# Turning x by a VectorE transpose of reloaded quarters instead of TensorE transposes, in a fused convolution and token-mixing kernel

## Chip, cores and metric

The kernel runs on one core of one Trainium2 chip. The metric is the device time of the core in microseconds (us), from the medians of several executions. Every execution that is used here was of the fast kind (no core at a reduced clock for the whole run), so all times can be compared.

## The reference

A causal convolution of seven taps along the tokens, one filter for each of eight channel groups, gives x. A channel product gives angles theta, their cosine and sine make a complex z, the tokens are mixed with two 4224x4224 weights, and a gated channel product ends it.

```python
# x: (8, 4224, 192); w: softmax of weight (8 heads, 7 taps)
x = causal_conv(x, w)                       # along the 4224 tokens
theta = x @ w_theta                         # 192 x 192
zr, zi = x * cos(theta), x * sin(theta)
y = einsum('ts,bsd->btd', w_tok_r, zr) + einsum('ts,bsd->btd', w_tok_i, zi)
u = x + y
out = u + maximum(u @ w_ch, 0)
```

## The kernel before

Tokens are cut into 33 chunks of 128. Only 11 chunks of z fit on the chip at a time, so the token mixing makes three passes over the outputs, and chunks 11 to 32, called the later chunks, are made in twelve *transition steps*, six in each of the two changes from pass to pass. There are 58 steps in all; a step mixes the live chunks into two blocks of 128 output tokens. It has seven runs of matmuls named `y` (seven products of half-width blocks in place of eight), and "position 3" in a step means "at the start of its fourth run". The work of a new chunk is slipped between the `y` matmuls at such positions. TensorE takes its instructions in program order, so what is slipped in must be ready when its turn comes.

The parts that the change touches (cuts are marked `# ...`):

```python
class Chunk:
    def conv(self, j):
        # ... 8 matmuls into pc, evicted into self.x (128 x 1536, by batch and channel)
        if j == 1:
            for a in range(NQ):                       # x is also kept in DRAM
                nc.sync.dma_start(out=xs[t0 : t0 + Q, :],
                                  in_=self.x[a * Q : (a + 1) * Q, :])

    def transpose(self, g):                           # 6 TensorE transposes, ACT evicts
        self.xT[g] = transposed(self.x[:, g * GC : (g + 1) * GC], ...)

    def theta(self, g):                               # 8 matmuls v, then Sin twice
        v = channel_mix(self.xT[g], wth)
        # ...

    def tasks(self):                                  # of one later chunk, in order
        # conv 0, conv 1, transpose 0, transpose 1, theta 0, theta 1, products, sums

class Step:
    def wtile(self):                                  # turned and summed weights
        return wpool.tile([P, NW, NQ, Q], F16, name="wt", tag="wt", bufs=11)

    def output(self, i, g):                           # out = u + relu(u @ w_ch)
        u = self.pv[i][:, g * GC : (g + 1) * GC]
        ub = u.rearrange("p (k n) -> p k n", k=2)
        dve(nc.vector.scalar_tensor_tensor(
            out=ub, in0=channel_mix(self.uT[i, g], wch), scalar=0.0, in1=ub,
            op0=ALU.max, op1=ALU.add))
        nc.sync.dma_start(out=out[...], in_=u...)     # leaves from pv itself

def step_events(t):
    # ...
    if t + 4 < NSTEP and steps[t + 4].late:           # x added into part, in DRAM
        for i in range(len(steps[t + 4].tbs)):
            found.append((3.3 + 1.7 * i, lambda i=i: steps[t + 4].add_ahead(i)))
    # ...
            pos = [0, .5, 1.3, 1.6, 2.1, 2.5, 3.1, 3.15, 3.4, 3.6]   # of tasks()
            # ... one chunk, then at += 2.3 for the second of the step
```

## Time and profile before

| | before |
|---|---|
| time, median | 1480.96 us of 3 runs (1479.57 to 1488.54) |
| span of the profile | 1482.4 us |
| start, to the first convolution of a later chunk | 108.4, then 315.0 us of pure token mixing |
| first transition (T1), 423.4 to 576.4 | 153.0 us |
| middle run of token mixing | 295.9 us |
| second transition (T2), 872.3 to 1020.0 | 147.7 us |
| rest, with the outputs | 462.4 us |

The lengths of stretches are differences of times in the timeline: a transition runs from its first convolution `pc` to its last theta matmul `v`.

The profile page of before, from its parts on busy time, on slices (a fortieth of the span each; digits are tenths, PEclk is the clock granted to TensorE) and on the chain that ended last:

```profile
PE 1434.0 (97%) x10095; PEld 904.5 (61%) x10095; DVE 859.6 (58%) x914; ACT 467.3 (32%) x597; POOL 522.2 (35%) x769
...
PE   7789999999999999999999999999999999969997
...
PEclk9999999999999999999999999999999999989999
...
PE 88%; DMA 4%; ACT 3%; DVE 2%; issue 1%; POOL 1%; SPq 0%; DVEq 0%; ACTq 0%; POOLq 0%
```

TensorE (PE) is busy 97% of the span, and the chain of work that ended last is 88% TensorE. VectorE (DVE) is busy 58% of the time. The one weak slice after the start, a 6 in the last third, is a gap. TensorE's waits in the whole of before (microseconds in all, times, longest):

```profile
engine line waited for: us in total, times, longest us
PE y L430 <- ACT pv L393: 14.5, 2, 13.7
...
PE v L138 <- ACT z L233: 3.0, 9, 0.6
```

The gap is the first line's 13.7 us, at 1321 us: a `y` product waits for ScalarE's eviction into `pv`, and ScalarE in turn waits 19.8 us for an output DMA that still reads the old `pv`.

The timeline of TensorE in before, in the first transition step (start, microseconds, engine, line, operation, operands, count):

```profile
425.61 0.52 PE L196 MATMUL pc<-xw,bands 96*64 96x192 f16 x8
...
428.35 0.50 PE L153 MATMUL tp<-ident,z 128*128 128x128 f16 x6
428.69 1.14 PE L430 MATMUL y<-z,wt 128*128 128x384 f16 x6
...
431.30 0.82 PE L138 MATMUL v<-wth,uT 128*128 128x192 f16 x8
```

Theta follows the end of the convolution's matmuls by about 5 us. And six transposes, given as 0.50 us, delay the next `y` by only 428.69 - 428.35 = 0.34 us, since matmuls overlap.

The same transitions in the table of stretches (stretch, length, busy time of each engine with its count, mean granted clock, share of the DMA engines, GB/s):

```profile
core 0: us, PE busy (x) PEld busy (x) DVE busy (x) ACT busy (x) POOL busy (x), PEclk, DMA share, GB/s
423.40:576.40 153.00, 153.00 (x1217) 98.50 (x1217) 95.35 (x117) 86.00 (x110) 56.26 (x93) 1.00 0.96 162
872.30:1020.00 147.70, 147.22 (x1181) 94.84 (x1181) 92.81 (x114) 84.02 (x108) 55.85 (x91) 1.00 1.02 172
```

The DMA share is the sum of the times of all packets over that of the 16 engines, so it can pass 1. In both stretches TensorE is busy with hardly a pause (0.5 us in the second) at full clock, and the DMA share is about 1.

### The profile page before, as it was taken

What the parts mean: (1) busy time and instruction counts of PE and PEld (TensorE: products, weight loads), DVE (VectorE), ACT (ScalarE), POOL (GpSimd) and SP (SyncE); (2) the same over time, 40 slices, a digit from 0 to 9 for tenths busy, and PEclk for the clock granted to TensorE, in tenths of its full rate; (3) what the DMA queues carried; (4) which work ended last, traced back from release to release, by engine and by line L of the source; (5) the groups of instructions that cost most, each with busy time, mean ns of one, the idle gap of its engine ahead of it and who ended that gap; (6) DMA issues with size and microseconds to landing.
All of it is one profiled execution on the core that took longest, in us unless ns stands there. A gap on an engine that the chain in (4) does not pass through costs nothing.

```text
span 1482.4 us, 24605 instructions
## 1 busy us (share of the span) xinstructions
PE 1434.0 (97%) x10095; PEld 904.5 (61%) x10095; DVE 859.6 (58%) x914; ACT 467.3 (32%) x597; POOL 522.2 (35%) x769
## 2 busy tenths in 40 slices
PE   7789999999999999999999999999999999969997
PEld 4556666666666666666666666666666666646664
DVE  6884554554547576545454547568556555545685
ACT  5861101011145454111111135464233333312334
POOL 7422211111323432222222333432455455564320
PEclk9999999999999999999999999999999999989999
DMA  9976756565789998868686899999898999999973
GB/s 169 240 151 144 142 114 132 103 143 100 144 155 151 189 151 153 140 104 138 104 136 108 126 178 144 186 160 161 144 184 184 189 181 225 197 253 206 275 190 108
DMA packets 234402, 237.22 MB, mean 160 GB/s; under 512 B 69040, under 2 KB 208176, under 8 KB 234288
## 3 DMA queue, kind: packets, MB, share of 16 engines
q0 software_dynamic: 176000, 147.21, 67.4%
q1 hardware_dynamic: 58288, 88.43, 18.1%
q8 instruction: 79, 1.29, 0.3%
q14 instruction: 35, 0.29, 0.1%
HBM read 209.32 MB, written 109.71 MB: 215 GB/s over the span
## 4 chain that ended last, share of the span: by engine, by line
PE 88%; DMA 4%; ACT 3%; DVE 2%; issue 1%; POOL 1%; SPq 0%; DVEq 0%; ACTq 0%; POOLq 0%
PE y L430 79%; PE v L138 5%; PE tp L153 3%; PE pc L196 2%; ACT z L233 2%; DMA out_dram<-pv 1%; DMA xr<-xs 1%; DMA st<-in_moe_w_tok_i_dram 1%; DMA pv<-part 1%; DVE wt L307 1%; POOL pv L377 0%; DMA xw<-xw 0%; DVE pv L395 0%; ACT uT L148 0%; DMA wch<-in_moe_w_ch_dram 0%
## 5 line engine op out<-in xcount | busy, mean ns | idle before, releaser
L430 PE MATMUL y<-z,wt 128*128 128x384 f16 x7656 | 1296.2, 326 | 19.9 <-ACT pv L393 14.5
L430 PEld LDWEIGHTS <-wt 128*128 128x128 f16 x7656 | 737.9, 98 | 487.2 <-issue 23.2
L395 DVE TENSOR_TENSOR pv<-y,pv 128x768 f32<-128x768 f32 x188 | 179.4, 955 | 396.9 <-PE y L430 334.8
L393 ACT ACTIVATE pv<-y 128x768 f32<-128x768 f32 x202 | 164.0, 812 | 717.0 <-PE y L430 697.2
L307 DVE STREAM_TRANSPOSE wt<-st 128x1408 f16<-128x1408 f16 (+7 forms) x224 | 324.2, 1460 | 6.6 <-DMA st<-in_moe_w_tok_i_dram 5.7
L294 POOL DMA_DIRECT2D st<-in_moe_w_tok_i_dram x232 | 133.4, 583 | 495.4 <-DVE wt L307 485.7
L319 DVE TENSOR_TENSOR wt<-wt 128x1408 f16<-128x1408 f16 (+7 forms) x216 | 181.6, 841 | 27.7 <-PE y L430 21.3
L294 POOL DMA_DIRECT2D st<-in_moe_w_tok_r_dram x232 | 141.9, 699 | 153.7 <-DVE wt L307 149.7
L148 ACT ACTIVATE uT<-tp 128x768 f16<-128x768 f16 x127 | 102.5, 813 | 179.9 <-PE tp L153 176.7
L238 DVE TENSOR_TENSOR z<-z 128x1536 f16<-128x1536 f16 x66 | 60.6, 953 | 98.7 <-ACT z L233 98.7
L138 PEld LDWEIGHTS <-uT 128*128 128x128 f16 x1056 | 91.8, 98 | 26.2 <-issue 10.6
L377 POOL TENSOR_TENSOR pv<-pv,xr 128x768 f32<-128x768 f32 x44 | 80.8, 1836 | 67.5 <-DVE pv L395 29.8
L456 DVE SCALAR_TENSOR_TENSOR pv<-v,pv 128x768 f32<-128x768 f32 x66 | 62.9, 954 | 69.4 <-PE v L138 43.4
L183 POOL DMA_DIRECT2D xw<-in_x_dram x132 | 77.3, 598 | 69.9 <-DMA part<-pv 41.9
L369 POOL DMA_DIRECT2D part<-pv x46 | 41.1, 893 | 118.7 <-DVE pv L395 63.6
L244 DVE TENSOR_TENSOR z<-z 128x768 f16<-128x768 f16 x132 | 73.4, 556 | 6.2 <-PE v L138 0.6
L446 ACT ACTIVATE ub<-pv 128x768 f16<-128x768 f32 x66 | 54.7, 836 | 49.3 <-DVE pv L395 29.8
L233 ACT ACTIVATE z<-v,half_pi 128x768 f16<-128x768 f32 x66 | 59.6, 903 | 32.0 <-PE v L138 31.9
L148 ACT ACTIVATE z<-pc 128x768 f16<-128x768 f32 x65 | 53.0, 815 | 23.1 <-PE pc L196 23.1
L138 PE MATMUL v<-wch,uT 128*128 128x192 f16 x528 | 55.2, 249 | 4.0 <-DVE pv L456 2.0
L138 PE MATMUL v<-wth,uT 128*128 128x192 f16 x528 | 54.4, 246 | 3.1 <-ACT z L233 3.0
L233 ACT ACTIVATE z<-v 128x768 f16<-128x768 f32 x66 | 53.2, 806 | 0.0
(45 smaller groups left out, 271.6 us busy)
## 6 DMA issues: line engine op xcount, KB each, us to landing
part<-pv POOLq DMA_DIRECT2D x46, 768.0 KB, 7.1
part<-pv SPq DMA_DIRECT2D x33, 768.0 KB, 4.1
out_dram<-pv SPq DMA_DIRECT2D x66, 384.0 KB, 4.8
st<-in_moe_w_tok_r_dram POOLq DMA_DIRECT2D x136, 176.0 KB, 7.3
st<-in_moe_w_tok_i_dram POOLq DMA_DIRECT2D x136, 176.0 KB, 4.7
pv<-part POOLq DMA_DIRECT2D x44, 384.0 KB, 6.8
xs<-z SPq DMA_DIRECT2D x132, 96.0 KB, 4.8
xw<-in_x_dram POOLq DMA_DIRECT2D x121, 96.0 KB, 6.0
```

The costliest lines, as they stand in the source:

```text
L138: pe(nc.tensor.matmul(v[:, k, b * D : (b + 1) * D], lhsT=tT[:, 3 * k + b + i, :], rhs=w[:, 2 * b + i, :], start=(i == 0), stop=(i == 1),))
L148: act(nc.scalar.activation(out=out, in_=in_, func=AT.Copy))
L183: nc.gpsimd.dma_start(out=self.xw[lo : lo + n, h, :, :], in_=x[:, t0 : t0 + n, :].rearrange("b s d -> s b d"),)
L233: act(nc.scalar.activation(**args))
L244: dve(nc.vector.tensor_tensor(out=z[:, o, :], in0=z[:, a, :], in1=z[:, b, :], op=ALU.subtract))
L294: pool(nc.gpsimd.dma_start(out=st[a * Q : (a + 1) * Q, 0:nb, :, 0:n] .rearrange("i r bt s -> i (r bt) s"), in_=w[self.tbs[0] * P : (self.t ...
L307: dve(nc.vector.transpose(self.w[name][:, 0 : self.n, :, :], self.st[int(name[1])][:, int(name[0]) - 1, :, 0 : self.n * Q] .rearrange("p b ...
L319: dve(nc.vector.tensor_tensor(out=self.w[name][:, 0 : self.n, :, :], in0=self.w[a][:, 0 : self.n, :, :], in1=self.w[b][:, 0 : self.n, :, : ...
L377: pool(nc.gpsimd.tensor_tensor(out=to, in0=to, in1=self.xr[i, j], op=ALU.add))
L393: act(nc.scalar.activation(out=o, in_=yv, func=AT.Copy))
L395: dve(nc.vector.tensor_tensor(out=o, in0=yv, in1=o, op=ALU.add))
L430: pe(nc.tensor.matmul(y[cn][:, q, 0:BH], lhsT=self.w[wn][:, c, :, :].rearrange("p bt i -> p (bt i)"), rhs=chunks[k].z[:, zn, q * BH : (q + ...
```

## The change

The intent is to take work from TensorE, which bounds the kernel, and to give it to engines with room. The columns of x are laid out by channel quarters. A VectorE transpose turns blocks of 32x32 only; the Trainium skill says so ("VectorE: DVE Perf Modes", The three transpose paths), so the blocks themselves must be brought to the right partitions in some other way. Here it is the rows that x writes to DRAM anyway: four DMAs reload them by quarters into `xq`, and one VectorE transpose of 128x1536 makes `xT`. This is done for the 22 later chunks; the first 11 still use TensorE, from a copy `xk` that VectorE puts into order.

In the quarters layout the last sum has three free dimensions, for which the compiler refuses the fused VectorE operation. So ScalarE takes the relu into an own buffer `ob`, and VectorE adds `pv`. The weight tiles `wt` go from 11 to 9 buffers to make room, and the positions of a new chunk's tasks change.

```diff
@@ Chunk
+        def load_quarters(self):
+            self.xq = wk.tile([P, NQ, NB], F16, name="xq", tag="wide")
+            for q in range(NQ):
+                nc.sync.dma_start(
+                    out=self.xq[q * Q : (q + 1) * Q, :, :],
+                    in_=xs[:, q * NB : (q + 1) * NB].rearrange(
+                        "(a k i) n -> k i a n", a=NQ, i=Q
+                    )[self.k, :, :, :],
+                )
+
+        def turn(self):
+            self.xT = turned("xT")
+            dve(nc.vector.transpose(
+                self.xT[:, :, :].rearrange("p k (a i) -> p k a i", a=NQ),
+                self.xq[:, :, :].rearrange("p a (k j) -> p k a j", j=Q),
+            ))
@@ tasks
-            for g in range(NG):
-                yield lambda g=g: self.transpose(g)
+            yield self.load_quarters
+            yield self.turn
@@ wtile
-  name="wt", tag="wt", bufs=11)
+  name="wt", tag="wt", bufs=9)
@@ output
-            dve(nc.vector.scalar_tensor_tensor(
-                out=ub, in0=channel_mix(self.uT[i, g], wch), scalar=0.0, in1=ub,
-                op0=ALU.max, op1=ALU.add,
+            ob = wk.tile([P, GC], F32, name="ob", tag="wide")
+            v = channel_mix(self.uT[i][:, 6 * g : 6 * g + 6, :], mixer["wch"])
+            act(nc.scalar.activation(
+                out=ob[:, :].rearrange("p (k n) -> p k n", k=2), in_=v, func=AT.Relu
+            ))
+            oq = ob[:, :].rearrange("p (b q c) -> p b q c", b=GB, q=NQ)
+            dve(nc.vector.tensor_tensor(
+                out=oq, in0=oq, in1=self.pv[i]..., op=ALU.add,
@@ step_events
-                pos = [0, .5, 1.3, 1.6, 2.1, 2.5, 3.1, 3.15, 3.4, 3.6]
+                pos = [0, .4, .45, 3, 3.5, 4, 4.6, 4.65, 4.95, 5.25]
@@
-                at += 2.3
+                at += 1.5
# cut: the column order in conv, theta, product, give and cast; the copy xk;
# the loads of wth and wch; buffers shared by xk, xq and ob (two, tag "wide"), by xr and
# ub (three); earlier positions for the outputs of all but the last six steps
```

More of the change, by code (lines that the diff above doesn't have):

```diff
@@ L58 @@
     GC = GB * D
+    DQ = D // NQ
+    NB = N // NQ
+    BQ = NB // NG
     BH = HN // 2
@@ L118, with new_mixer, load_channel_weights @@
     ident = constp.tile([P, P], F16, name="ident")
-    R = D - P
-    wth = constp.tile([P, 4, D], F16, name="wth")
-    wch = constp.tile([P, 4, D], F16, name="wch")
-    def channel_pieces(w):
-        return ((slice(0, P), 0, w[0:P, :]), (slice(0, R), 1, w[P:D, :]),
-                (slice(R, P), 2, w[0:R, :]), (slice(0, P), 3, w[R:D, :]))
+    mixer = {}
+    def new_mixer(name):
+        mixer[name] = constp.tile([P, 4, D], F16, name=name, tag="mixer")
+        return mixer[name]
+    def load_channel_weights(dma, t, w):
+        for q in range(NQ):
+            lo, d = q * Q, q * DQ
+            for to, rows, n in ((t[lo : lo + Q, 0, :], d, Q),
+                                (t[lo : lo + DQ - Q, 1, :], d + Q, DQ - Q),
+                                (t[lo + DQ - Q : lo + Q, 2, :], d, 2 * Q - DQ),
+                                (t[lo : lo + Q, 3, :], d + DQ - Q, Q)):
+                dma(out=to, in_=w[rows : rows + n, :])
     def token(k, a):
@@ L148, in evacuate, with transposed @@
             act(nc.scalar.activation(out=out, in_=in_, func=AT.Copy))
-    def transposed(u, by_dve=False):
+    def transposed(uT, u, by_dve=False):
         tp = banks("tp", F16)
@@ L155, in transposed, with turned @@
             ))
-        uT = wk.tile([P, 6, P], F16, name="uT", tag="uT")
-        evacuate(uT[:, :, :].rearrange("p k s -> p (k s)"), tp[:, 0, 0 : 6 * P], by_dve)
-        return uT
+        evacuate(uT.rearrange("p k s -> p (k s)"), tp[:, 0, 0 : 6 * P], by_dve)
+    def turned(name):
+        return wk.tile([P, 12, P], F16, name=name, tag="turned")
     Z11, T1, Z21, Z22, T2, T4, T3 = range(7)
@@ L196, in conv @@
                     pe(nc.tensor.matmul(
-                        pc[half * 2 * Q : (half + 1) * 2 * Q, h // 2,
-                           h % 2 * B * G : (h % 2 + 1) * B * G],
+                        pc[half * 2 * Q : (half + 1) * 2 * Q, h // 2, 0:NB]
+                        .rearrange("p (b h g) -> p b h g", b=B, h=2)[:, :, h % 2, :],
                         lhsT=bands[:, 4 * j + h, :, :].rearrange("p a m -> p (a m)"),
@@ L203, in conv @@
             evacuate(
-                self.x.rearrange("p (b d) -> p b d", d=D)[
-                    :, :, 4 * j * G : 4 * (j + 1) * G
-                ].rearrange("p b (i h g) -> p i h b g", i=2, h=2),
-                pc[:, :, 0 : 2 * B * G].rearrange("p i (h b g) -> p i h b g", h=2, b=B),
+                self.x[:, j * HN : (j + 1) * HN].rearrange("p (q n) -> p q n", q=2),
+                pc[:, :, 0:NB],
                 self.k == 0 and j == 1,
@@ L217, in transpose @@
         def transpose(self, g):
-            self.xT[g] = transposed(
-                self.x[:, g * GC : (g + 1) * GC], 0 < self.k < 3 or (self.k, g) == (0, 1)
-            )
+            if g == 0:
+                self.xT = turned("xT")
+                self.xk = wk.tile([P, N], F16, name="xk", tag="wide")
+                dve(nc.vector.tensor_copy(
+                    out=self.xk[:, :].rearrange("p (k q j) -> p k q j", q=NQ, j=Q),
+                    in_=self.x.rearrange("p (q k j) -> p k q j", q=NQ, j=Q),
+                ))
+            transposed(
+                self.xT[:, 6 * g : 6 * g + 6, :], self.xk[:, g * GC : (g + 1) * GC],
+                0 < self.k < 3 or (self.k, g) == (0, 1),
+            )
+        def load_quarters(self):
+            self.xq = wk.tile([P, NQ, NB], F16, name="xq", tag="wide")
+            for q in range(NQ):
+                nc.sync.dma_start(
[5 more added lines that the diff above has]
+        def turn(self):
+            self.xT = turned("xT")
+            dve(nc.vector.transpose(
+                self.xT[:, :, :].rearrange("p k (a i) -> p k a i", a=NQ),
+                self.xq[:, :, :].rearrange("p a (k j) -> p k a j", j=Q),
+            ))
         def theta(self, g):
-            v = channel_mix(self.xT[g], wth).rearrange(
-                "p k (b h e) -> p k b h e", b=2, h=2
+            v = channel_mix(self.xT[:, 6 * g : 6 * g + 6, :], mixer["wth"]).rearrange(
+                "p k (b q c) -> p k b q c", b=2, q=NQ
             )
             for first, bias in ((Z11, half_pi[:]), (Z21, None)):
-                o = self.z[:, first : first + 2, :].rearrange(
-                    "p h (k b e) -> p k b h e", b=2, e=HD
+                o = self.z[:, first : first + 2, :].rearrange("p t n -> p (t n)").rearrange(
+                    "p (q k b c) -> p k b q c", q=NQ, b=2, c=DQ
                 )[:, 2 * g : 2 * g + 2, :, :, :]
@@ L235, in product @@
         def product(self, first):
-            o = self.z[:, first : first + 2, :].rearrange("p h (b e) -> p h b e", e=HD)
-            xv = self.x.rearrange("p (b h e) -> p h b e", h=2, e=HD)
-            dve(nc.vector.tensor_tensor(out=o, in0=xv, in1=o, op=ALU.mult))
+            o = self.z[:, first : first + 2, :].rearrange("p t n -> p (t n)")
+            dve(nc.vector.tensor_tensor(out=o, in0=self.x, in1=o, op=ALU.mult))
         def sums(self, which):
@@ L302, in wtile @@
         def wtile(self):
-            return wpool.tile([P, NW, NQ, Q], F16, name="wt", tag="wt", bufs=11)
+            return wpool.tile([P, NW, NQ, Q], F16, name="wt", tag="wt", bufs=9)
         def turn(self, name):
@@ L355, in load_x @@
         def load_x(self, i, j):
-            self.xr[i, j] = wk.tile([P, HN], F16, name="xr", tag="xr", bufs=2)
+            self.xr[i, j] = wk.tile([P, HN], F16, name="xr", tag="half", bufs=3)
             nc.sync.dma_start(
@@ L387, in give @@
         def give(self, y, i, h, opens):
-            o = self.pv[i][:, :].rearrange(
-                "p (q b h e) -> p q b h e", q=2, h=2, e=HD
-            )[:, :, :, h, :]
-            yv = y[:, :, 0:BH].rearrange("p q (b e) -> p q b e", e=HD)
+            o = self.pv[i][:, h * HN : (h + 1) * HN].rearrange("p (q n) -> p q n", q=2)
+            yv = y[:, :, 0:BH]
             if opens and not self.late:
@@ L444, in cast @@
         def cast(self, i, g):
-            self.ub[i, g] = wk.tile([P, GC], F16, name="ub", tag="ub", bufs=2)
+            self.ub[i, g] = wk.tile([P, GC], F16, name="ub", tag="half", bufs=3)
             act(nc.scalar.activation(
-                out=self.ub[i, g], in_=self.pv[i][:, g * GC : (g + 1) * GC], func=AT.Copy
+                out=self.ub[i, g][:, :].rearrange("p (k q j) -> p k q j", q=NQ, j=Q),
+                in_=self.pv[i][:, :].rearrange("p (q k j) -> p k q j", q=NQ, j=Q)[
+                    :, 6 * g : 6 * g + 6, :, :
+                ], func=AT.Copy,
             ))
         def turn_u(self, i, g):
-            self.uT[i, g] = transposed(self.ub[i, g])
+            if g == 0:
+                self.uT[i] = turned("uT")
+            transposed(self.uT[i][:, 6 * g : 6 * g + 6, :], self.ub[i, g])
         def output(self, i, g):
-            u = self.pv[i][:, g * GC : (g + 1) * GC]
-            ub = u.rearrange("p (k n) -> p k n", k=2)
-            dve(nc.vector.scalar_tensor_tensor(
-                out=ub, in0=channel_mix(self.uT[i, g], wch), scalar=0.0, in1=ub,
-                op0=ALU.max, op1=ALU.add,
+            ob = wk.tile([P, GC], F32, name="ob", tag="wide")
+            v = channel_mix(self.uT[i][:, 6 * g : 6 * g + 6, :], mixer["wch"])
+            act(nc.scalar.activation(
+                out=ob[:, :].rearrange("p (k n) -> p k n", k=2), in_=v, func=AT.Relu
+            ))
+            oq = ob[:, :].rearrange("p (b q c) -> p b q c", b=GB, q=NQ)
+            dve(nc.vector.tensor_tensor(
+                out=oq, in0=oq, in1=self.pv[i][:, :].rearrange(
+                    "p (q b c) -> p b q c", q=NQ, c=DQ
+                )[:, g * GB : (g + 1) * GB, :, :], op=ALU.add,
             ))
@@ L462, in output @@
                 out=out[g * GB : (g + 1) * GB, rows, :].rearrange("b s d -> s b d"),
-                in_=u.rearrange("p (b d) -> p b d", d=D),
+                in_=ob[:, :].rearrange("p (b d) -> p b d", d=D),
             )
@@ L473, in outputs @@
                 else:
-                    at = 9.5 + 10 * i
-                    every, turn, mix = 4.0, 2.9, 4.7
+                    at = 8.5 + 8 * i
+                    every, turn, mix = 3.4, 2.5, 4.2
                 for g in range(NG):
@@ L508, in step_events, with load_wch @@
                 found.append((7 * begin / steps[t].time, f))
+        if t == start[-1]:
+            def load_wch():
+                wch = new_mixer("wch")
+                dve(nc.vector.memset(wch[:, 1:3, :], 0.0))
+                load_channel_weights(nc.gpsimd.dma_start, wch, moe_w_ch)
+            found.append((0.5, load_wch))
         if t >= NU - 2:
@@ L524, in step_events @@
                     add(at + p, j, k)
-                at += 2.3
+                at += 1.5
         return found
     load_chunk(0)
-    stage = [wk.tile([P, 2, D], F32, name="stage", tag="ub", bufs=2) for _ in range(2)]
-    for i in range(2):
-        nc.vector.memset(stage[i][:, 1 - i, :], 0.0)
-    for rows, i, part_w in channel_pieces(moe_w_theta):
-        nc.sync.dma_start(out=stage[i // 2][rows, i % 2, :], in_=part_w)
+    stage = wk.tile([P, 4, D], F32, name="stage", tag="big", bufs=6)
+    nc.vector.memset(stage, 0.0)
+    load_channel_weights(nc.sync.dma_start, stage, moe_w_theta)
     noise = zpool.tile([P, BH], F16, name="noise", tag="z")
@@ L603 @@
     ))
-    for i in range(2):
-        dve(nc.vector.tensor_copy(out=wth[:, 2 * i : 2 * i + 2, :], in_=stage[i]))
+    dve(nc.vector.tensor_copy(out=new_mixer("wth"), in_=stage))
     def stream():
@@ L676 @@
         between(1)
-    nc.vector.memset(wch[:, 1:3, :], 0.0)
-    for rows, i, part_w in channel_pieces(moe_w_ch):
-        nc.gpsimd.dma_start(out=wch[rows, i, :], in_=part_w)
     ready[0] = NK
```

## The prediction

> **What bounds the kernel.** TensorE: the profile page has PE busy 1434 of 1482 us (97%), and the chain of work that ended last is 88% PE, 79% the token matmuls `y` (7656). VectorE (58%) and ScalarE (32%) have room. By the table of stretches PE idles at the start (busy 89 of 111 us), at the end (21 of the last 33), and, by the waits, in one gap of 13.7 us at 1321 us, where ScalarE's eviction into `pv` waits 19.8 us for an output DMA that still reads the old `pv`. There the granted clock falls to 0.50, as the Trainium skill ("TensorE: Matmul & The Clock Gate", part 1) says of idle windows of about 3.4 us; long gaps cost more than their length.
>
> **Removed.** For 22 later chunks, 12 TensorE transposes each. In the timeline six transposes delay the next `y` by 0.34 us: 15 us of PE time, all critical. Also 44 ScalarE evictions of 0.81 us, not critical. Outputs now leave from their own buffer, so `pv` is free at the VectorE add, not at the landing: the gap (about 15 us with the clock) should mostly go.
>
> **Added.** A VectorE transpose of 128x1536 per later chunk, about 1.8 us by the 1.63 us of 128x1408 (39 us, affordable). A relu on ScalarE per output, 66 x about 0.8 us. A copy per early chunk on VectorE (86% busy there): a few us at the start. At the end the output chain gets one more link, and two output buffers wait for landings: +2 to 5 us.
>
> **The risk: the reload's latency.** In a transition step (12 in all) the first chunk's x goes to DRAM and back before VectorE can turn it, and TensorE takes its theta matmuls in order. By the order listing 56 `y` and two convolutions stand between: about 10 us. Before, the first chunk's writes of `xs` land 7 to 9 us after issue in nearly every such step, later ones in 2 to 4.6. Eviction 0.9 + issue 1.4 + landing 7 + reload issue 1.5 and landing 2.5 to 4 + turn 1.8 is 15 to 17 us against 10. Fewer weight buffers (9 for 11) delay the turn that frees the staging buffer by about 1.5 us, so the weight loads may collide less with the write and more with the reload. I estimate 1 to 6 us of PE stall per step, about 40 in all.
>
> **Sum.** 1481 - 15 - 15 + 5 (start, end) + 25 = 1481; I take less than my estimate of the stall, because the new positions look tuned to hide it. Predicted 1480 us, range 1450 to 1530; faster by over 2% 0.15, within 2% 0.52, slower 0.33.
>
> **What would show it.** Groups: 528 PE transposes for 792, and 22 VectorE transposes of 128x1536 near 1.8 us. Waits: TensorE `v` for VectorE `xT`, and `xT` for DMA `xq`, in 12 places from 420 to 575 and 870 to 1015 us; if each is under 0.5 us the risk was wrong and the time is near 1455. The gap at 1321 us gone, or replaced by ScalarE `ob` waiting for output DMAs. Landings of `xq` and of the first `xs`.
>
> **What would make it wrong.** DMA traffic shifted so that write and reload land in 2 to 3 us each (faster); clock drops in every stall (slower); output buffers blocking ScalarE, so that evictions into `pv` come late and stop TensorE in the last third; fewer weight buffers making VectorE late for the adds into `pv`.

## The result

The changed kernel is correct and slower: 1605.51 us median of 4 runs (1604.02 to 1606.72) against 1480.29 us of the kernel before in the same rounds (4 runs, 1479.57 to 1488.54). The ratio is 1.0832, with a 95% interval of 1.0791 to 1.0872. A ratio here and below is the mean time of one kernel's fast runs over that of the other's of the same rounds, so it is not quite the ratio of the medians that are quoted.

The page of after, the same parts as of before:

```profile
PE 1456.2 (91%) x9831; PEld 906.9 (57%) x9831; DVE 928.8 (58%) x945; ACT 486.0 (30%) x619; POOL 527.0 (33%) x781
...
PE   7899999999977778999999987777799999998996
...
PEclk9999999999988889999999998888899999999998
...
PE 73%; DMA 13%; DVE 5%; ACT 4%; SPq 2%; issue 2%; POOL 1%; DVEq 0%; ACTq 0%; POOLq 0%
```

TensorE is busy 22 us more, though transposes were taken from it, and its share of the span falls from 97% to 91%. The two dents are the two transitions: the busy digits fall to 7 and the clock digits to 8. DMA has 13% of the chain for 4%. TensorE's waits in after:

```profile
PE v L151 <- DVE xT L257: 104.4, 13, 11.5
PE tp L167 <- ACT ub L483: 9.9, 6, 4.2
PE tp L167 <- DVE xk L234: 8.8, 10, 2.5
```

The first line did not exist in before: 104.4 us of waiting for VectorE's turned `xT`, in 13 places. The gap of 13.7 us is gone; shorter waits for the cast `ub` of outputs and for the copy `xk` of early chunks took places of their own. The two transitions in the table of stretches:

```profile
core 0: us, PE busy (x) PEld busy (x) DVE busy (x) ACT busy (x) POOL busy (x), PEclk, DMA share, GB/s
427.50:639.00 211.50, 162.96 (x1098) 99.62 (x1098) 114.10 (x126) 69.96 (x88) 57.21 (x94) 0.88 0.79 140
932.90:1144.70 211.80, 155.81 (x1054) 95.73 (x1054) 112.84 (x124) 68.60 (x87) 58.07 (x95) 0.85 0.81 144
```

Stretch by stretch, after minus before: start +4.1, first mixing 0.0, T1 211.5 - 153.0 = +58.5, middle -2.0, T2 211.8 - 147.7 = +64.1, rest 459.9 - 462.4 = -2.5. The sum is 122.2 us, the difference of the spans; 122.6 of it lie in the transitions. What holds TensorE there is shown by the chain of waits of after, in order of time (start, microseconds, what). It is cut to the first transition step:

```profile
429.94 0.82 ACT z L161
...
430.77 0.32 SPq L226
...
431.61 0.74 SPq L226
...
432.39 6.03 DMA xs<-z
...
438.48 0.32 SPq L248
...
439.79 4.46 DMA xq<-xs
...
444.37 1.79 DVE xT L257
...
446.20 1.46 PE v L151 x8
```

ScalarE evicts x, the sync engine issues four writes, and they land 6.03 us after the last issue began (the chain counts a landing from there). Only then may the reload be issued; it lands 4.46 us after its last issue began, VectorE turns it in 1.8 us, and theta starts at 446.20. From the end of the convolution (429.94 by the start of the eviction) this is 16.3 us. The `y` matmuls between were used up at 440.2, so TensorE stands still:

```profile
435.17 5.05 PE L467 MATMUL y<-z,wt 128*128 128x384 f16 x30
446.20 1.46 PE L151 MATMUL v<-wth,xT 128*128 128x192 f16 x8 [5.99 <-DVE xT L257]
447.46 2.77 PE L467 MATMUL y<-z,wt 128*128 128x384 f16 x8
```

This is the timeline of TensorE in after; the bracket is the wait of 5.99 us. After it, the eight theta matmuls take 1.46 us where before they took 0.82, as at half the clock. The Trainium skill says that TensorE falls to half rate after an idle window of about 3.4 us and needs about as long again to recover ("TensorE: Matmul & The Clock Gate", Part 1). The trace agrees with the half rate: asked in half microseconds, the table of stretches gives 1.00 until 4.6 us after TensorE stopped and then 0.50. It stays so for the first 5.4 us of the work after the wait, 446.2 to 451.6; over the twelve steps this is 3.1 to 6.0 us, mostly longer than the page's figure.

The chain over both transitions, of which the ninth step is shown:

```profile
1009.77 10.32 DMA xs<-z
1021.55 4.35 DMA xq<-xs
```

Over the twelve steps, it gives 5.8 to 10.3 us for the write (median of 12: 7.4) and 2.2 to 5.9 us for the reload (median of 11: 4.9; one step's chain goes another way). These figures hold the time of the last issue too. The timeline of the sync engine in the ninth step shows how long the four issues of each take:

```profile
1007.75 4.76 SPq L226 DMA_DIRECT2D xs<-z  x4
1020.23 1.76 SPq L248 DMA_DIRECT2D xq<-xs  x4
```

Counted so in all twelve steps, the four issues of the write take 2.1 to 4.8 us (median 3.2) and the landing 4.8 to 7.6 us after their end (median 6.0). The four issues of the reload take 1.7 to 2.3 us and the landing 1.8 to 5.5 us (median 4.5). The whole, from the eviction to theta, is 16.3 to 21.0 us, 18.6 in the mean.

The Trainium skill gives a DMA a fixed cost of about 2.0 us, mostly the receipt of the write ("DMA: Bandwidth & Descriptors", Anatomy of one DMA, for transfers issued by GpSimd). These land next to the transfers that GpSimd issues, the weight loads among them, and most take far longer: the DMA share is 1.0 to 1.3 while the writes are under way and 0.6 to 1.5 during these reloads. The reloads of the second chunks of the same steps, at a share of 0.4 to 0.5, land in 1.7 to 3.2 us (median 1.8). The stalls of the twelve first chunks are 6.0 to 11.5 us.

The clock's part can be worked out. TensorE's busy time in the transitions rose from 300.2 to 318.8 us (T1 and T2 added), by 18.6. The transposes that left should have lowered it by 44 x 0.34 = 15, and 18 `y` that moved into the stretches (1446 for 1428 records) raise it by 18 x 0.163 = 2.9. So 18.6 + 15 - 2.9 = 30.7 us of busy time are more than the work needs: an estimate of the loss at half clock. Another way agrees: after the twelve stalls TensorE worked 58 us in all at a granted clock of 0.50, which loses half of that, 29 us. Waits and busy time together, 104.4 + 18.6 = 123 us, are the 122.6 by bookkeeping; that sum is no test.

Last, the output add, as the view of tile `ob` in after gives it (minimum, median and maximum in ns):

```profile
L502 DVE TENSOR_TENSOR ob<-ob,pv x66: 915/958/3166, 1187.3 to 1600.1; 128x768 f32<-128x768 f32 x66
```

Its mean is 1216 ns by the page, where the fused operation on PSUM took 954 in before. The timeline shows why the two differ: the ten adds of 2143 to 3166 ns are those that overlap one of GpSimd's adds `pv<-pv,xr`, and the other 56 take 915 to 959. The fused operations of before that overlap such an add took 947 to 958. So the split, which makes both inputs of VectorE's add SBUF tiles, also let GpSimd hold it up.

### The profile page after: what moved, and what is told of

Its sections match the earlier page's. It is cut to its first block, busy times and chain, and to the rows that moved or that the text cites. A ratio compares the mean times of both kernels' runs of the same rounds, so it can differ in the third digit from the quotient of the medians.

```text
span 1604.6 us, 24254 instructions
## 1 busy us (share of the span) xinstructions
PE 1456.2 (91%) x9831; PEld 906.9 (57%) x9831; DVE 928.8 (58%) x945; ACT 486.0 (30%) x619; POOL 527.0 (33%) x781
## 4 chain that ended last, share of the span: by engine, by line
PE 73%; DMA 13%; DVE 5%; ACT 4%; SPq 2%; issue 2%; POOL 1%; DVEq 0%; ACTq 0%; POOLq 0%
PE y L467 65%; DMA xs<-z 6%; PE v L151 5%; DMA xq<-xs 3%; DVE xT L257 2%; SPq L226 2%; DMA out_dram<-ob 1%; PE tp L167 1%; ACT z L273 1%; ACT z L161 1%; PE pc L211 1%; SPq L248 1%; DMA st<-in_moe_w_tok_r_dram 1%; DVE pv L432 1%; ACT ob L498 1%
## 5 line engine op out<-in xcount | busy, mean ns | idle before, releaser
L467 PEld LDWEIGHTS <-wt 128*128 128x128 f16 x7656 | 746.5, 99 | 489.5 <-issue 21.1
L358 DVE TENSOR_TENSOR wt<-wt 128x1408 f16<-128x1408 f16 (+7 forms) x216 | 188.3, 872 | 124.7 <-PE y L467 120.2
L151 PE MATMUL v<-wth,xT 128*128 128x192 f16 x528 | 68.3, 285 | 106.5 <-DVE xT L257 104.4
L502 DVE TENSOR_TENSOR ob<-ob,pv 128x768 f32<-128x768 f32 x66 | 80.3, 1216 | 130.4 <-ACT ob L498 130.2
L151 PEld LDWEIGHTS <-xT 128*128 128x128 f16 x528 | 54.5, 114 | 123.5 <-DVE xT L257 110.3
L257 DVE STREAM_TRANSPOSE xT<-xq 128x1536 f16<-128x1536 f16 x22 | 38.7, 1759 | 110.5 <-DMA xq<-xs 69.0
L498 ACT ACTIVATE ob<-v 128x768 f32<-128x768 f32 x66 | 53.5, 810 | 82.3 <-PE v L151 41.4
L161 ACT ACTIVATE uT<-tp 128x768 f16<-128x768 f16 x66 | 53.2, 809 | 48.5 <-PE tp L167 48.1
```

The lines of the kernel that those rows point to most:

```text
L151: pe(nc.tensor.matmul(v[:, k, b * D : (b + 1) * D], lhsT=tT[:, 3 * k + b + i, :], rhs=w[:, 2 * b + i, :], start=(i == 0), stop=(i == 1),))
L161: act(nc.scalar.activation(out=out, in_=in_, func=AT.Copy))
L358: dve(nc.vector.tensor_tensor(out=self.w[name][:, 0 : self.n, :, :], in0=self.w[a][:, 0 : self.n, :, :], in1=self.w[b][:, 0 : self.n, :, : ...
L467: pe(nc.tensor.matmul(y[cn][:, q, 0:BH], lhsT=self.w[wn][:, c, :, :].rearrange("p bt i -> p (bt i)"), rhs=chunks[k].z[:, zn, q * BH : (q + ...
L502: dve(nc.vector.tensor_tensor(out=oq, in0=oq, in1=self.pv[i][:, :].rearrange("p (q b c) -> p b q c", q=NQ, c=DQ)[:, g * GB : (g + 1) * GB, ...
```

## The experiments

The theory: TensorE waits in order for the reload (T1 and T2), and the half clock after each wait adds a quarter more. The rivals: fewer weight buffers, the new positions, or the longer output path. Fourteen kernels ran, each with the kernel before on the same chip. All but the two that read other rows gave the reference's result.

### e1_pe_turns: the changed kernel with TensorE's turning and the old positions for later chunks

```diff
-            yield self.load_quarters
-            yield self.turn
+            for g in range(NG):
+                yield lambda g=g: self.transpose(g)
...
-                pos = [0, .4, .45, 3, 3.5, 4, 4.6, 4.65, 4.95, 5.25]   # at += 1.5
+                pos = [0, .5, 1.3, 1.6, 2.1, 2.5, 3.1, 3.15, 3.4, 3.6] # at += 2.3
```

> Everything of the change but the reload: later chunks are turned on TensorE again, at the old positions; quarters, output buffer, relu on ScalarE and 9 weight buffers stay. Theory A (the round trip of x through DRAM, with the clock it costs, makes the whole loss of 125 us): 1475 to 1490 us, no wait of v for xT over 1 us, the two transition stretches back at about 153 and 148 us. Rival B (fewer weight buffers, or the layout and ScalarE's relu, delay VectorE and with it TensorE): 1550 us or more.

Measured: 1528.27 us, ratio 1.0311 [1.0279, 1.0343]. The waits for `xT` are gone and 77 us are won, but 46 over its own before are left. Nearly all of it lies in the transitions, which take 344.4 us for 300.7. TensorE's waits in e1 between 400 and 1080 us:

```profile
PE tp L167 <- DVE xk L234: 30.5, 10, 4.4
```

The transposes need the copy `xk` from VectorE. VectorE takes its work in order too, and the copy stands behind sums of weights that wait for a weight buffer, which TensorE frees. Besides the 31 us of waits, TensorE is busy 13 us longer in the transitions, at a mean clock of 0.95 and 0.98. So the expectation was missed: the round trip through DRAM is the greater part, but an in-order step on VectorE in TensorE's path costs as well. That the nine buffers have a part in it is argued, not tested: e1 with eleven was not run.

### e2_stale_rows: the reload reads rows written a pass earlier (wrong)

```diff
-                    )[self.k, :, :, :],
+                    )[self.k - NW, :, :, :],
```

> Wrong on purpose: the reload reads the rows of the chunk eleven before, long written, so it waits for no write and can be issued ahead; size, queue and VectorE's turn stay as in the change. Theory A: the stalls (104 us) and the half clock after them (about 33 us) go, 1460 to 1475 us. Rival C (the load on VectorE and the DMA traffic of the turn itself delay TensorE, not the wait for the write): over 1540 us, waits of v for xT still some us each.

Measured: 1492.75 us, ratio 1.0065 [1.0038, 1.0091]; the result is wrong. The same DMAs, the same VectorE turn and the same positions are there, but the reload need not wait for this chunk's write. The transitions in e2, columns as above, and its waits:

```profile
429.40:584.00 154.60, 149.29 (x1097) 91.48 (x1097) 113.41 (x126) 69.97 (x88) 57.25 (x94) 1.00 1.07 190
878.00:1031.70 153.70, 143.61 (x1053) 88.13 (x1054) 113.21 (x125) 69.08 (x87) 58.04 (x95) 0.99 1.09 194
```

```profile
PE v L151 <- DVE xT L257: 14.7, 15, 4.4
```

The stalls fall from 104.4 to 14.7 us and the clock is back at 1.00 and 0.99. So the wait for the fresh rows, with what it starts, makes 1605.5 - 1492.8 = 113 of the 125 us. All rivals together (nine buffers, positions, layout, output path) are still in this kernel, and it is about 10 us over before. The 1460 to 1475 us that I had expected were missed: the turn still stands behind VectorE's weight sums (longest wait 4.4 us), and the start is 6 us longer than before's. This suggests what is to be had by hiding the reload at these positions: about before's time. The test moves the loads too: the scheduler put them up to a step ahead. So it takes away the whole round trip, and does not part the write from the reload.

### e3_before_wt9: before, with 9 weight buffers

```diff
-  name="wt", tag="wt", bufs=11)
+  name="wt", tag="wt", bufs=9)
```

> The kernel before with 9 instead of 11 weight buffers, nothing else. Theory A: within 1% of before (1475 to 1495 us). Rival B: a loss of 40 us or more, with VectorE's turns late and the adds into pv holding TensorE.

Measured: 1483.23 us, ratio 1.0007 [0.9968, 1.0045]. Nine buffers alone cost nothing, so this rival falls as a cause by itself. They are not without effect: in the first transition VectorE's weight work waits 43.3 us for TensorE in e3 and 3.7 in before. In this kernel TensorE's path to theta does not go through VectorE, so it costs nothing; in e1 and in the change it does.

### e4_keep_warm: the changed kernel with 44 useless matmuls before the first theta of each transition step

```diff
         def theta(self, g):
+            if g == 0 and self.leads:
+                dummy = banks("dummy")
+                for _ in range(44):
+                    pe(nc.tensor.matmul(
+                        dummy[:, 0, 0:BH], lhsT=ident, rhs=self.x[:, 0:BH],
+                        start=True, stop=True))
```

> The changed kernel with 44 useless matmuls of 128x384 (about 7 us) ahead of the first theta of each transition step, where TensorE waits anyway. If a stall costs its length plus the time at half clock after it, this ADDS work and is faster: 1570 to 1590 us, granted clock near 1 in both transitions. If the granted clock plays no part: 1605 us or more.

Measured: 1588.45 us, ratio 1.0708 [1.0676, 1.0740], 17 us faster than the changed kernel, with 528 matmuls more. The transitions in e4:

```profile
427.00:640.00 213.00, 205.14 (x1432) 124.95 (x1431) 123.81 (x139) 73.43 (x92) 59.07 (x96) 0.99 0.83 148
930.00:1150.00 220.00, 207.48 (x1415) 126.74 (x1414) 129.63 (x143) 70.01 (x88) 67.08 (x114) 0.97 0.82 143
```

The clock rises from 0.88 and 0.85 to 0.99 and 0.97, and 20.4 us of waiting for `xT` are left. (The windows are wider than the transitions, which take 203.4 and 202.5 us from the first convolution to the last theta.) The matmuls fill time that is lost anyway, and keep the rate. This shows the clock's part of the loss by intervention: 17 us won of the 30 worked out. Three of the twelve steps still have a stretch at half clock, and in some the fill was longer than the wait.

### e5_before_ob: before, with an own output buffer (and 9 weight buffers for its room)

```diff
+            ob = wk.tile([P, GC], F32, name="ob", tag="ob", bufs=2)
             dve(nc.vector.scalar_tensor_tensor(
-                out=ub, in0=channel_mix(self.uT[i, g], wch), scalar=0.0, in1=ub,
+                out=ob..., in0=channel_mix(self.uT[i, g], wch), scalar=0.0, in1=ub,
...
-                in_=u.rearrange("p (b d) -> p b d", d=D),
+                in_=ob[:, :].rearrange("p (b d) -> p b d", d=D),
```

> The kernel before (TensorE turns, old layout) with 9 weight buffers and only one piece of the change: the output leaves from its own two-fold buffer, written by the same single VectorE operation. If the gap of 13.7 us at 1321 us is caused by pv being held until its output DMA has landed: the gap is gone, 1463 to 1473 us. If saturated DMA would have stopped TensorE there anyway: 1480 us, with the wait at another place.

Measured: 1485.19 us, ratio 1.0002 [0.9979, 1.0025]. No gain: the wait for the output DMA went, and another took its place. Followed `y` by `y` in the two traces, e5 is 2.7 us behind before when it reaches the gap, 4.9 ahead after it and 2.6 ahead from 1403 us on; 2.5 of the lag come from the start, unexplained. All waits of e5 between 1290 and 1400 us, its two lines of interest:

```profile
ACT ub L446 <- DMA pv<-part: 21.6, 4, 9.8
...
PE tp L153 <- ACT ub L446: 5.0, 1, 5.0
```

TensorE now waits 5.0 us for the cast `ub`, which waits for the DMA that accumulates `part` into `pv`. My forecast of 15 us from freeing `pv` early was wrong: the DMA share is 1.05 to 1.14 there, and the next DMA is late as well.

### e6_before_ob_relu: e5 with the relu on ScalarE and the add on VectorE

```diff
-            dve(nc.vector.scalar_tensor_tensor(..., op0=ALU.max, op1=ALU.add))
+            act(nc.scalar.activation(
+                out=ov, in_=channel_mix(self.uT[i, g], wch), func=AT.Relu))
+            dve(nc.vector.tensor_tensor(out=ov, in0=ov, in1=ub, op=ALU.add))
```

> As the run beside it, but relu on ScalarE into the output buffer and then VectorE's add, as in the change. If ScalarE's longer queue gave back what the gap would have returned in the last third of the change: 8 to 14 us slower than the run beside it, with waits of TensorE for ub and a longer end. If the relu on ScalarE is harmless: within 3 us of it.

Measured: 1491.14 us, ratio 1.0043 [1.0018, 1.0068] on the chip where e5 took 1485.19. Splitting the fused operation costs about 6 us, between the two forecasts and a small part of the 125. Here too VectorE's add is slow beside GpSimd's: 13 of the 66 overlap one and take 1.3 to 3.0 us, the others 0.91 to 0.96. How much of the 6 us this makes was not tested.

### e7_sbuf_sp: no DRAM, 16 small transfers within SBUF for each chunk

```diff
+                for a in range(NQ):
+                    nc.sync.dma_start(
+                        out=self.xq[q * Q : (q + 1) * Q, a, :],
+                        in_=self.x[a * Q : (a + 1) * Q, q * NB : (q + 1) * NB])
```

> The changed kernel, but xq is filled straight from x in SBUF by 16 small transfers of 24 KB a chunk on the same queue (8 after each convolution half), not from DRAM: correct, and no wait for the landing of the write. Theory A says that the write's landing (6 to 9 us) is most of the stall: issue of 16 takes about 6 us, so turns come 0 to 3 us late; 1490 to 1525 us. If the DMA engines are simply full at that time, so that any transfer lands late: stalls stay at 5 us or more, over 1550 us.

Measured: 1662.90 us, ratio 1.1201 [1.1171, 1.1231], far from the expectation and the slowest of all. The timeline of the sync engine in e7, first transition step:

```profile
429.12 11.43 SPq L253 DMA_DIRECT2D xq<-z  x16
...
440.59 1.99 SPq L228 DMA_DIRECT2D xs<-z  x4
...
442.68 10.01 SPq L253 DMA_DIRECT2D xq<-z  x16
```

Sixteen issues take 11.43 us, longer than the landing that they were to save, and the second chunk's wait behind the first's. TensorE waits 143.1 us for `xT`. The Trainium skill calls the time to initiate a DMA "usually small relative to the DMA itself" ("DMA: Bandwidth & Descriptors", Issuing engines are not separate DMA queues). For one piece this holds in the trace: 0.59 us (median) against 3.9 from issue to landing. But sixteen in order add up.

### e8_sbuf_sp_act: the same, half of the transfers issued by ScalarE

```diff
-                    nc.sync.dma_start(
+                    (nc.sync if a < 2 else nc.scalar).dma_start(
```

> As the run beside it, but half of the 16 small transfers are issued by ScalarE's queue, so that issue takes half as long. If issue is what is left of the stall: faster than the run beside it by 5 to 20 us. If VectorE's wait for a weight buffer ahead of the turn is what is left: the same within 5 us.

Measured: 1584.05 us, ratio 1.0665 [1.0638, 1.0693]. TensorE's waits in e8:

```profile
PE y L470 <- ACT pv L433: 55.7, 12, 7.2
PE v L151 <- DVE xT L260: 34.2, 15, 11.3
```

The wait for `xT` falls to 34.2 us, but ScalarE, held up by issuing (median 0.60 us each), evicts late, and TensorE waits 55.7 us for that. The loss moved; it was not removed.

### e9_ahead: the convolution of a later chunk one step earlier

The convolution writes its rows to DRAM in the step before, and the transition step reloads both the rows and the quarters. The core of the edit:

```diff
+            for at, k in zip((3.6, 4.2), new):              # one step ahead
+                found.append((at, lambda k=k: chunks[k].conv_ahead(0)))
+                found.append((at + .4, lambda k=k: chunks[k].conv_ahead(1)))
+                found.append((at + .45, lambda k=k: chunks[k].load_quarters()))
...
-            for j in range(2):
-                yield lambda j=j: self.conv(j)
-            yield self.load_quarters
+            yield self.load_rows
             yield self.turn
```

> The changed kernel, but the convolution of a later chunk runs one step earlier into a buffer of its own, is written and read back by quarters during the rest of that step, and its plain rows are read back too once z is free: more DMA traffic, but a whole step for the round trip, and VectorE's turn stands ahead of the sums that wait for a weight buffer. Theory A (only the time between write and turn is missing): no wait of v for xT over 1 us, transition stretches near 140 us, 1465 to 1480 us. If the DMA traffic itself is too much: waits of v or pc for xw or xT of several us in each step, over 1500 us.

Measured: 1561.19 us, ratio 1.0513 [1.0483, 1.0544]: 44 us faster than the changed kernel, and a miss. Waits for `xT` of 64.8 us in 11 places are left. In the first step the second chunk's `xq` was issued at 432.42 us, right after VectorE had finished the first chunk's turn: `xq` has only two buffers, shared with `ob` and here with the early x, so an earlier write brought no earlier reload for it. The landing then took 6.69 us. In e9 waits of 2.7 and 3.0 us left theta at 0.83 us, and those of 4.5 us and more made it 1.46.

### e10_ahead_stt4: e9 with four fused VectorE operations for each output, no ScalarE relu

```diff
-            act(nc.scalar.activation(..., func=AT.Relu))
-            dve(nc.vector.tensor_tensor(out=oq, in0=oq, in1=..., op=ALU.add))
+            for b in range(GB):                             # one batch at a time
+                dve(nc.vector.scalar_tensor_tensor(
+                    out=ob[...], in0=v[...], scalar=0.0, in1=self.pv[i]...,
+                    op0=ALU.max, op1=ALU.add))
```

> As the run beside it, and relu and add in one VectorE operation per batch (four an output, since one takes at most two free dimensions) in place of ScalarE's relu and VectorE's add. If the longer ScalarE chain costs the end and the last third some us: 4 to 10 us faster than the run beside it. If four short VectorE operations cost as much as they save: within 3 us of it.

Measured: 1561.81 us, ratio 1.0504 [1.0465, 1.0543], the same as e9 within the intervals. Four small operations with the relu are worth as much as two large ones. Each took 324 to 359 ns, beside GpSimd's adds too.

### e11_stale_early: e2 with the old early positions (wrong)

```diff
-                    )[self.k, :, :, :],
+                    )[self.k - NW, :, :, :],
...
-                pos = [0, .4, .45, 3, 3.5, 4, 4.6, 4.65, 4.95, 5.25]
+                pos = [0, .4, .45, 1.3, 2.1, 2.5, 3.1, 3.15, 3.4, 3.6]
```

> Wrong on purpose, as the run with stale rows, and VectorE's turn moved ahead of the sum that waits for a weight buffer (first chunk at 1.4 sevenths of the step, second at 2.9), theta and the rest back at about the old positions. If the 15 us of waits left in the run with stale rows come from the turn standing in VectorE's order behind a sum that waits for TensorE to free a weight buffer: these waits fall under 4 us in all and the transition stretches to about 140 us each, 1465 to 1480 us. If VectorE is just too slow: no change, 1490 us.

Measured: 1522.51 us, ratio 1.0276 [1.0245, 1.0308]. The positions are about the old ones, not quite. It was to show that e2's small waits come from the turn's place in VectorE's order. In the first step, where the data was there, theta did not wait at all. In others the loads were late and 31.2 us of waits in six places appeared. The test is inconclusive for the whole kernel; it does show that, with stale rows, the later positions are 30 us better than these. The positions were not tested by themselves in the changed kernel.

### e12_before_add10 and e13_before_ob_add10: x added to the late blocks ten steps ahead, without and with the own output buffer

These and e14 ask why e5 gained nothing. In the last third many DMAs meet: x is added into `part` for the late blocks, in DRAM, while the outputs leave.

```diff
-        if t + 4 < NSTEP and steps[t + 4].late:
-            for i in range(len(steps[t + 4].tbs)):
-                found.append((3.3 + 1.7 * i, lambda i=i: steps[t + 4].add_ahead(i)))
+        if t + 10 < NSTEP and steps[t + 10].late:
+            for i in range(len(steps[t + 10].tbs)):
+                found.append((3.3 + 1.7 * i, lambda i=i: steps[t + 10].add_ahead(i)))
```

> The kernel before, but the additions of x to the stored partial sums for the last six steps are issued ten steps ahead, not four, so they leave the stretch from 1230 to 1390 us where the DMA engines are full. If the gap at 1321 us comes from full DMA engines: it shrinks to under 3 us and the time is 1465 to 1473 us. If it comes only from pv being held by its output: unchanged, 1480 us.

> The same, together with the own output buffer and 9 weight buffers: 1460 to 1472 us if both causes add, the same as the run beside it if the full DMA engines were the only cause.

Measured: e12 1486.04 us, ratio 1.0025 [0.9994, 1.0055]; e13 1479.20 us, ratio 0.9972 [0.9936, 1.0008]. In e12 the gap shrinks to 6.95 us and new waits of 2.3 and 2.7 us appear where the additions went. In e13 the gap is gone, and waits of 1.95 and 2.12 us stand near 1153 and 1215 us, where the DMA share is now 1.11. The crowd was moved, not thinned.

### e14_ob_spread: e5 with one block of additions in each of twelve steps

```diff
+        for i, n in ((0, 11), (1, 5)):
+            if t + n < NSTEP and steps[t + n].late and i < len(steps[t + n].tbs):
+                found.append((3.3, lambda i=i, n=n: steps[t + n].add_ahead(i)))
# in place of both blocks of a step together, four steps ahead
```

> A version that may beat both: the kernel before with the own output buffer and 9 weight buffers, and the additions of x to the stored partial sums spread, one block a step over twelve steps (first blocks 11 steps ahead, second blocks 5), in place of two a step over six. If full DMA engines in the last third make the remaining waits: the gap at 1321 us is gone and the waits near 1153 and 1215 us of the run with ten steps ahead are under 1 us each, 1466 to 1476 us. If not: within 0.3% of before.

Measured: 1470.74 us against 1486.46 of before in the same rounds, ratio 0.9895 [0.9865, 0.9926]. It is correct, as forecast in time, and beats both kernels; the gain is 1%, within the 2% called the same, but the interval leaves out 1. The stretches from 1130 to 1330 us, first of before and then of e14:

```profile
1130.00:1230.00 100.00, 100.00 (x727) 65.76 (x726) 56.15 (x51) 32.22 (x41) 53.55 (x55) 1.00 0.95 187
1230.00:1330.00 100.00, 90.94 (x655) 59.40 (x653) 54.88 (x49) 28.47 (x36) 61.25 (x68) 0.97 1.05 223
```

```profile
1130.00:1230.00 100.00, 100.00 (x727) 65.76 (x726) 56.00 (x51) 32.21 (x41) 57.90 (x60) 1.00 1.03 210
1230.00:1330.00 100.00, 100.00 (x724) 65.51 (x722) 57.62 (x53) 32.14 (x41) 57.22 (x62) 1.00 1.06 221
```

The DMA share of before was 0.95 and then 1.05; spread, it is 1.03 and 1.06, and TensorE is busy without a pause in both. The share is not lower on the whole, but even; that no single DMA in TensorE's path comes late any more is how I read it. The own buffer alone (e5) gained nothing, moving the additions alone (e12) nothing. Spreading without the own buffer was not run.

## Why the prediction was wrong

- **The mechanism was right.** The waits named (TensorE's `v` for `xT`, `xT` for `xq`) came in the windows named. e2 takes the wait for fresh rows away (and so lets the loads go out earlier), keeps all else, and brings 113 of the 125 us back.
- **The step that failed is the size of the stall.** The prediction put it: "I estimate 1 to 6 us of PE stall per step, about 40 in all", and in the sum "25 ... I take less than my estimate of the stall, because the new positions look tuned to hide it". Measured: 104.4 us of waits, 8.7 for each of twelve steps. Its own chain of "15 to 17 us against 10" would have given 5 to 7 us, 60 to 84 in all. The chain was right in the first step (16.3 us, 10.3 covered) and short for the others: 17.5 to 21.0 us, with 10.1 to 10.3 us of cover in all but the last, where it was 6.4. In the mean it is 18.6 us: the write took 9.6 (3.4 for the four issues, 6.2 for the landing) where "issue 1.4 + landing 7" stood, and the reload 6.1 (1.8 and 4.3) where "1.5 and landing 2.5 to 4" stood.
- **The clock was named and left out of the sum.** "Clock drops in every stall (slower)" was listed as what would make it wrong. All twelve stalls, 6.0 to 11.5 us long, ended at half clock, and the loss is about 30 us by two estimates; e4 confirms its kind and won 17 us back.
- **The gap's 15 us were won and lost again.** The rest of the kernel is only 2.5 us shorter, and e5 shows no gain from this part alone. Followed `y` by `y`, the lag of after behind before falls from 124 to 110 us across the gap and is 117 again within 40 us, where TensorE waits 4.2 us for the cast `ub` and ScalarE, before it, 11.7 us for the DMA that adds `part` into `pv`. Behind the first cause stood a second, the late accumulation into `pv`. In e14 TensorE waits for neither there.
- **What was right.** 528 transposes for 792, a VectorE turn of 1.76 us (forecast 1.8), +4.1 us at the start, and the gap at 1321 gone.
- **What stays open.** e1 left 46 us over before, with waits for the copy `xk` measured at 30.5 us in the transitions; nine buffers alone are harmless in before (e3), but their part in e1 was only argued from VectorE's order and its waits. And no version kept the VectorE turn and reached before's time: earlier writes (e9) ran into the two shared buffers.

With what was measured the sum would have been 1481 - 15 + 4 (start) + 3 (moved `y`) + 104 + 31 - 2.5 (rest) - 2 (middle) = 1603.5, for 1605.5. This is bookkeeping that shows which terms were mis-sized, not a test.

## What to carry to other kernels

Where an in-order engine must wait for data that goes to DRAM and back, take the loaded latency of write, reload and both issues from the trace of that very stage, multiply it by the number of places, and do not shorten it because positions look tuned. "Issue the DMA early, do compute" (the Trainium skill, "DMA: Bandwidth & Descriptors", Rules for kernel authors) holds only if the cover is counted: here it was 10 us of `y` for a chain of 16 to 21. A stall on TensorE of 6 us or more cost its length and then 3 to 6 us at half rate here; and an engine that is half idle is not free if its order puts the new work behind a wait.

## What the Trainium skill lacked or had wrong

- "DMA: Bandwidth & Descriptors" (Anatomy of one DMA; Latency and other measured facts) gives a fixed cost of about 2 us and says that HBM answers more slowly at high load, but has no landing time for a transfer issued by the sync engine while another queue keeps the DMA engines busy. Here four writes of 96 KB took 2.1 to 4.8 us to issue and landed 4.8 to 7.6 us after that, and the first chunks' reloads landed after 1.8 to 5.5 us. A table of issue and landing time by load would have helped here.
- The same page (Issuing engines are not separate DMA queues) calls the issue time usually small, which holds for one transfer. It does not say that issues add up on their engine: 0.43 us (median) for a reload of 96 KB and 0.59 us for a small SBUF to SBUF transfer, 11.4 us for sixteen in a row; on ScalarE (0.60 us) they kept evictions waiting.
- "TensorE: Matmul & The Clock Gate" (HAM oscillation) tells of idle gaps, and its rules of warm-up matmuls for benchmarks, but not that useless matmuls in a wait that can't be avoided pay: 528 of them made the kernel 17 us faster (e4).
- "VectorE: DVE Perf Modes" (The three transpose paths) gives 390 ns for a 128x128 transpose on TensorE (the TensorE page about 275 ns in one kernel), without what it takes of TensorE's time in a stream of matmuls. Here six took 0.34 us of TensorE's time, 57 ns each, so for a bound TensorE the price to save is a seventh of that.
- Not lacking: "SBUF — State Buffer" (Who interferes with whom) says that a VectorE instruction with two SBUF inputs contends with a GpSimd instruction that reads SBUF. The trace agrees: of 66 adds of 128x768, the ten beside GpSimd's adds took 2143 to 3166 ns and the others 915 to 959.
